# Staging the transposed attention weights: three buffers instead of two, one of them inside freed memory, and the pieces spread evenly over nineteen chunks

## The chip, the cores and the metric

The kernel runs on one core of a Trainium2 chip. The metric is device time in microseconds (us) of one execution. Before the change the median of eight executions is 3200.1 us (3193.46 to 3205.57). One execution was recorded by the hardware profiler; all rows of the profile below are from it.

The engines are named as in the profile: PE is TensorE's matmul, PEld its weight load, DVE is VectorE, ACT is ScalarE, POOL is GpSimd, SP is SyncE. SP, ACT and POOL also issue DMA transfers: the hardware queues of SP and ACT appear as q1 and q10, the software queue of POOL as q0.

## The reference, cut to what matters

The kernel computes the output and all gradients of one transformer block: a conditioned layer norm, recurrent attention over 64 segments of 32 tokens that carry 8 memory rows, a second conditioned layer norm, and a gated linear unit (GLU).

```python
# forward
h = layernorm(x) * (1 + ca) + sa
x = x + ga * attention(h, mem0, Wq, Wk, Wv, Wo)     # 64 segments, one after another
h2 = layernorm(x) * (1 + cb) + sb
hh = sigmoid(h2 @ w_gate) * (h2 @ w_up)
out = x + gb * (hh @ w_down)
# backward, the parts near the change (grad_out is given)
d_w_down = hh.T @ d_b                               # out_9
d_w_gate = h2.T @ d_g ;  d_w_up = h2.T @ d_u        # out_7, out_8
# and then the attention, from the last segment to the first; it needs
# Wo, Wv, Wk and Wq transposed
```

Sizes: 2048 tokens, model width 512, 32 heads of 128, GLU width 1792. Everything is bfloat16, and the sums are float32.

## The kernel before, in words

The program has phases: the forward attention (`phase2`), the GLU forward and backward by tiles of 128 tokens and after them the GLU's weight gradients (`phase3`), the backward attention (`phase4`), and the attention's weight gradients (`phase5`). The change lies in the last part of `phase3`, which the profile shows from about 1391 to 1587 us.

**The chunks.** This part computes weight gradients as long sums on TensorE: each output tile sums 16 matmuls, one for each tile of 128 tokens. First come eleven chunks of the gradient of `w_down` (fc = 3 to 13; `wd_chunk`, matmuls on L1141), each of 16 matmuls of 512 columns. Then come eight chunks of the GLU weight gradients (four of `w_gate`, four of `w_up`; L1211), each of 4 x 16 matmuls of 448 columns. That makes `n_chunks` = 19.

**The rings.** The operands are loaded into memory that the forward attention has left. `Wk` holds `dbr` in one half and `h2r` in the other. `Wv` (16384 elements per partition) holds a ring of two halves of 7168 elements: the chunks of HHROWS (1.5 MB), then of DGROWS and DUROWS (1.8 MB each). Their loads are issued on the ACT queue (L1137, L1187), each when the chunk that last read that half is done. The 2048 elements of `Wv` behind the ring are not used in this part. In the GLU tiles ahead they held two buffers of `grad_out` and two of the attention's rows.

**The pieces.** The backward attention needs `WoT`, `WvT`, `WkT` and `WqT`. `p4_weights_setup_pieces` makes 32 pieces, eight for each matrix in that order. A piece loads 0.5 MB of weights into a stage buffer (the load on L1265 or L1279), turns it with 16 transposes on TensorE in four groups of four (L1270 or L1283), and copies each group from PSUM with DVE or ACT (L63, L61). PSUM has two buffers for the groups (`wtp`). The stage pool has two buffers, so the load of a piece waits until the piece two before it has been turned. All 32 loads run on SP's queue, since `kk` is a multiple of 4 whenever a load is issued.

**The order.** After each chunk `emit_setup` emits two pieces until none is left: 22 behind the eleven chunks of `w_down`, and 10 behind the first five GLU chunks. The last three GLU chunks have none. The framework fixes each engine's order when the kernel is built: it takes instructions by their emission order and readiness, and an engine then executes its list strictly in that order. A group of transposes whose load is late therefore holds the matmuls listed behind it. The framework also sets the waits: a write into memory waits for the accesses before it that overlap it, and a new tile waits until the tiles that had the memory are released.

**Around it.** The store of the last tile of the GLU part (`DAOT`, L1121) and a reload from it (`daq`, L1243) are on SP's queue among the first piece loads. The first copy into `WoT` takes memory that this store reads. At the end the pools are closed, and the buffers of `phase4` (loads on L1405, L1408 and L1422, memsets on L1333, `RBd`, `dOT`) take the memory of `Wv`, `Wk` and the stages.

Of the kernel before, what the change touches and what calls it, by code (L numbers as in the profile page):

```python
# [7 lines left out]
BF16 = mybir.dt.bfloat16  # L8
# [32 lines left out]
class K:  # L41
# [856 lines left out]
    def phase3(self):  # L898
        nc, tc, cfg, io = self.nc, self.tc, self.cfg, self.io
        D, DC, F, FC, NT, T = cfg.D, cfg.DC, cfg.F, cfg.FC, cfg.NT, cfg.T  # L900
# [6 lines left out]
        d = self.dram  # L907
        with ExitStack() as ctx:
# [224 lines left out]
            kk = [0]  # L1133

            def load_hr(g):
                w = min(384, F - 384 * g)
                (nc.sync if g < 2 else nc.scalar).dma_start(hrs[g][:, :, 0:w], self.HHROWS[:, 384 * g:384 * g + w].rearrange("(j p) f -> p j f", p=128))  # L1137

            def wd_chunk(fc, ps, ot):
                for j in range(NT):  # L1140
                    nc.tensor.matmul(ps[:], lhsT=hrs[fc // 3][:, j, (fc % 3) * 128:(fc % 3) * 128 + 128], rhs=dbr[:, j, :],  # L1141
                                     start=(j == 0), stop=(j == NT - 1))
                self.evac("act" if kk[0] % 2 == 0 else "dve", ot[:], ps[:])
                kk[0] += 1
                nc.gpsimd.dma_start(io["out_9"][fc * 128:(fc + 1) * 128, :], ot[:])
# [22 lines left out]
        with ExitStack() as ctx:  # L1168
            op_ = ctx.enter_context(tc.tile_pool(name="p3g_o", bufs=2, reuse_waits="tile"))
            psG = ctx.enter_context(tc.tile_pool(name="p3g_ps", bufs=4, space=PSUM, reuse_waits="tile"))  # L1170
            setup_pieces = self.p4_weights_setup_pieces(ctx)
            n_chunks = 2 * NCH + FC - 3
            per_chunk = (len(setup_pieces) + n_chunks - 1) // n_chunks

            def emit_setup():
                for _ in range(per_chunk):
                    if setup_pieces:
                        setup_pieces.pop(0)()
            h2r = self.flat(self.Wk, NT * D, NT * D).rearrange("p (j d) -> p j d", j=NT)
            load_hr(2)  # L1180
            xrs = []

            def load_xr(i):
                if i < 2 * NCH:
                    rows, ch = ((self.DGROWS, self.DUROWS)[i // NCH], i % NCH)
                    t = ring[i % 2].rearrange("p (j f) -> p j f", j=NT)
                    nc.scalar.dma_start(t, rows[:, ch * CH:(ch + 1) * CH].rearrange("(j p) f -> p j f", p=128))  # L1187
                    xrs.append(t)

            for fc in range(3, FC):  # L1190
                wd_chunk(fc, psG.tile([128, D], F32, name="gps2", tag="g"), op_.tile([128, D], BF16, name="ot2", tag="o"))
                if fc == 4:
                    self.get_db(cfg.NS // 4 - 1)
                if fc == 5:
                    load_hr(3)
                elif fc == 8:
                    load_hr(4)
                elif fc == 9:
                    nc.scalar.dma_start(h2r, self.H2ROWS[:, :].rearrange("(j p) d -> p j d", p=128))
                elif fc == 11:  # L1200
                    load_xr(0)
                emit_setup()
            load_xr(1)
            k = kk[0]
            for (rows, outw) in ((self.DGROWS, io["out_7"]), (self.DUROWS, io["out_8"])):
                for ch in range(NCH):
                    xr = xrs.pop(0)
                    for c in range(DC):
                        ps = psG.tile([128, CH], F32, name="gps", tag="g")
                        for j in range(NT):  # L1210
                            nc.tensor.matmul(ps[:], lhsT=h2r[:, j, c * 128:(c + 1) * 128], rhs=xr[:, j, :],  # L1211
                                             start=(j == 0), stop=(j == NT - 1))
                        ot = op_.tile([128, CH], BF16, name="ot", tag="o")
                        self.evac("act" if k % 2 == 0 else "dve", ot[:], ps[:])
                        k += 1
                        nc.gpsimd.dma_start(outw[c * 128:(c + 1) * 128, ch * CH:(ch + 1) * CH], ot[:])
                    load_xr(NCH * (outw is io["out_8"]) + ch + 2)
                    emit_setup()
            while setup_pieces:
                setup_pieces.pop(0)()  # L1220
# [31 lines left out]
    def p4_weights_setup_pieces(self, ctx):  # L1252
        nc, tc, cfg, io = self.nc, self.tc, self.cfg, self.io
        D, DC, H, E = cfg.D, cfg.DC, cfg.H, cfg.E
        HB = 4
        stg = ctx.enter_context(tc.tile_pool(name="p4stage", bufs=2, reuse_waits="tile"))
        sps = ctx.enter_context(tc.tile_pool(name="p4sps", bufs=2, space=PSUM, reuse_waits="tile"))
        pieces = []
        kk = [0]

        def qkv_piece(src_ap, dst, h0):
            def f():
                srcv = src_ap.rearrange("(c p) h e -> p c h e", p=128)
                wn = stg.tile([128, DC, HB, E], BF16, name="wn", tag="s")
                (nc.sync if kk[0] % 2 == 0 else nc.gpsimd).dma_start(wn[:], srcv[:, :, h0:h0 + HB, :])  # L1265
                for hi in range(HB):
                    h = h0 + hi
                    tp = sps.tile([128, DC, 128], BF16, name="wtp")
                    for c in range(DC):
                        nc.tensor.transpose(tp[:, c, :], wn[:, c, hi, :], self.ident[:])  # L1270
                    self.evac("dve" if kk[0] % 3 != 2 else "act", dst[:, h, :], tp[:, :, :].rearrange("p c d -> p (c d)"))
                    kk[0] += 1
            return f

        def wo_piece(h0):
            def f():
                wov = io["A_Wo"].rearrange("h e d -> e h d")
                won = stg.tile([128, HB, D], BF16, name="won", tag="s")
                (nc.sync if kk[0] % 2 == 0 else nc.gpsimd).dma_start(won[:], wov[:, h0:h0 + HB, :])  # L1279
                for c in range(DC):  # L1280
                    tp = sps.tile([128, HB, 128], BF16, name="wtp")
                    for i in range(HB):
                        nc.tensor.transpose(tp[:, i, :], won[:, i, c * 128:(c + 1) * 128], self.ident[:])  # L1283
                    self.evac("dve" if kk[0] % 3 != 2 else "act", self.WoT[:, c, h0 * E:(h0 + HB) * E],
                              tp[:, :, :].rearrange("p i e -> p (i e)"))
                    kk[0] += 1
            return f

        for h0 in range(0, H, HB):
            pieces.append(wo_piece(h0))  # L1290
        for (src_ap, dst) in ((io["A_Wv"], self.WvT), (io["A_Wk"], self.WkT), (io["A_Wq"], self.WqT)):
            for h0 in range(0, H, HB):
                pieces.append(qkv_piece(src_ap, dst, h0))
        return pieces
# [725 lines left out]
```

The softmax here doesn't subtract the row's maximum and nothing guards it: scores larger than these inputs give would overflow.

## Time and profile before

| what | value |
|---|---|
| median of eight executions | 3200.1 us |
| the profiled execution: time, span | 3197.22 us, 3195.4 us |
| PE busy | 2985.6 us (93% of the span) |
| DVE, ACT, POOL busy | 1586.9, 1159.0, 1481.2 us |
| mean granted TensorE clock | 0.982 of full speed |
| DMA in the whole span | 726.12 MB, mean 227 GB/s |
| chunks of `w_down` and first GLU matmuls, 1391 to 1485 us | 23.19 MB, mean 247 GB/s |
| rest of the GLU weight gradients, 1485 to 1587 us | PE without idle time |

Times in a row are microseconds unless they are marked ns. A row of the timeline gives the start, the time to the end of the merged instructions, the engine, the line, what is written and read, the count, and in brackets the idle time of the engine before it with what ended it. A group `x4` of transposes is one of the four groups of a piece.

### The profile page before, as it was taken

How to read it: one execution, taken by the hardware profiler on the slowest of the kernel's cores; microseconds unless marked ns; L12 is line 12 of the kernel's file. 1: busy time of each engine (PE TensorE's matmuls, PEld its weight loads, DVE VectorE, ACT ScalarE, POOL GpSimd, SP SyncE). 2: the span in 40 equal slices, each digit the busy share in tenths (PEclk: the TensorE clock that was granted, in tenths of full speed). 3: DMA queues.
4: the chain of work that ended last, by engine and by line, in shares of the span. 5: the costliest groups of instructions: out<-in, count | busy, mean ns of one | idle time of the engine just before them, and what ended most of it. 6: DMA issues, size and time to landing. Idle time of an engine off the chain costs nothing.

```text
span 3195.4 us, 98797 instructions
## 1 busy us (share of the span) xinstructions
PE 2985.6 (93%) x39993; PEld 1727.7 (54%) x40069; DVE 1586.9 (50%) x3770; ACT 1159.0 (36%) x2829; POOL 1481.2 (46%) x2973
## 2 busy tenths in 40 slices
PE   5999999999998899988989999999999969999999
PEld 3666666666665444445555555555555534455454
DVE  4655666666655777633244545555555521323221
ACT  2454444444444333312144444444444410101011
POOL 3666666666664566521244444444444421333322
PEclk8999999999999999989999999999999989999999
DMA  9888888888788798887599999999999999998886
GB/s 296 204 211 202 203 202 207 202 203 211 196 203 245 180 220 216 218 255 233 184 222 253 261 256 267 271 267 262 269 256 272 261 223 221 239 207 206 203 229 154
DMA packets 958893, 726.12 MB, mean 227 GB/s; under 512 B 656019, under 2 KB 831139, under 8 KB 958309
## 3 DMA queue, kind: packets, MB, share of 16 engines
q1 hardware_dynamic: 827940, 508.77, 70.5%
q0 software_dynamic: 59056, 148.62, 13.9%
q10 hardware_dynamic: 71440, 62.40, 7.7%
q8 instruction: 316, 5.18, 0.7%
q14 instruction: 141, 1.15, 0.1%
HBM read 294.91 MB, written 276.33 MB: 179 GB/s over the span
## 4 chain that ended last, share of the span: by engine, by line
PE 41%; DMA 8%; issue 4%; ACT 2%; DVE 1%; POOL 1%; SPq 1%; ACTq 0%; DVEq 0%; POOLq 0%
PE dh_ps L212 10%; PE gps L1813 5%; PE pass_ps L249 4%; PE gps5o L1826 4%; PE g_ps L1502 4%; PE gps L1211 3%; PE dh_tps L212 3%; DMA rows<-DKR 2%; PE tps L1417 2%; PE dp_ps L1481 1%; ACT RAd L61 1%; PE dp_ps L1489 1%; DMA Kst<-KST 1%; PE dh_ft L318 1%; PE turn_ps L1383 1%
## 5 line engine op out<-in xcount | busy, mean ns | idle before, releaser
L1813 PE MATMUL gps<-rows,hrows 128*128 128x512 bf16 (+2 forms) x2124 | 415.7, 355 | 3.8 <-ACT ot L61 1.9
L1813 PEld LDWEIGHTS <-hrows 128*128 128x128 bf16 x2160 | 211.1, 98 | 206.7 <-issue 2.3
L249 PEld LDWEIGHTS <-hT 128*32 128x32 bf16 x6144 | 158.1, 97 | 161.4 <-issue 1.9
L1531 POOL COPY dOst<-RAd 96x512 bf16<-96x512 bf16 x128 | 78.5, 614 | 358.4 <-DVE RAd L63 347.5
L852 POOL TENSOR_TENSOR Pst<-Pst,rden 120x1408 bf16<-120x1408 bf16 x63 | 161.0, 2555 | 112.3 <-issue 78.8
L1817 POOL DMA_DIRECT2D out_dram<-ot x108 | 81.5, 755 | 227.8 <-DVE ot L63 140.3
L63 DVE CAST ot<-gps 128x512 bf16<-128x512 f32 (+3 forms) x76 | 47.9, 632 | 249.1 <-PE gps L1813 105.9
L309 DVE TENSOR_TENSOR dh_lo<-dh_ps,dh_hi 128x256 bf16<-128x256 f32 x128 | 48.4, 420 | 246.0 <-ACT dh_hi L305 246.0
L1826 PE MATMUL gps5o<-WoT,rows 128*128 128x512 bf16 x588 | 133.7, 387 | 25.3 <-DMA rows<-OSR 24.6
L61 ACT ACTIVATE ot<-gps 128x512 bf16<-128x512 f32 (+3 forms) x75 | 41.0, 548 | 282.8 <-PE gps L1813 106.6
L212 PE MATMUL dh_ps<-WvT,dVT 128*32 128x512 bf16 x2048 | 135.1, 381 | 0.0
L249 PE MATMUL pass_ps<-Wv,hT 128*32 128x512 bf16 x2048 | 133.5, 380 | 0.0
L249 PE MATMUL pass_ps<-WoT,dyT 128*32 128x512 bf16 x2048 | 123.6, 384 | 5.2 <-ACT dyT L1590 5.2
L1491 DVE SCALAR_TENSOR_TENSOR dS<-dp_ps,Pst_l 128x512 bf16<-128x512 f32 (+1 forms) x192 | 112.2, 640 | 32.3 <-PE dp_ps L1489 32.2
L220 PE MATMUL at_ps<-Wo,OT 128*32 128x256 bf16 x4096 | 124.6, 275 | 0.5 <-DVE OT L63 0.2
L249 PE MATMUL pass_ps<-Wk,hT 128*32 128x512 bf16 x2048 | 123.2, 382 | 1.5 <-ACT hT L842 1.1
L212 PE MATMUL dh_ps<-WkT,dKT 128*32 128x512 bf16 x2048 | 124.0, 383 | 0.1
L212 PE MATMUL dh_ps<-WqT,dQT 128*32 128x512 bf16 x2048 | 122.3, 379 | 0.1
L249 PE MATMUL pass_ps<-Wq,hT 128*32 128x512 bf16 x2048 | 121.8, 379 | 0.0
L61 ACT ACTIVATE dVT<-g_ps 128x512 bf16<-128x512 f32 (+1 forms) x192 | 107.8, 562 | 37.3 <-PE g_ps L1502 18.3
L63 DVE CAST RA0v<-pass_ps 128x512 bf16<-128x512 f32 x128 | 88.3, 690 | 65.7 <-PE pass_ps L249 61.2
L694 ACT ACTIVATE ET<-st_ps 128x480 bf16<-128x480 f32 (+1 forms) x192 | 96.1, 535 | 54.2 <-ACT qT L61 37.3
(407 smaller groups left out, 7038.8 us busy)
## 6 DMA issues: line engine op xcount, KB each, us to landing
OSR<-Ost SPq DMA_DIRECT2D x64, 352.0 KB
OT<-OT SPq DMA_DIRECT2D x64, 352.0 KB
VT<-VTr SPq DMA_DIRECT2D x64, 352.0 KB
PS<-Pst SPq DMA_DIRECT2D x64, 352.0 KB
OT_l<-OT SPq DMA_DIRECT2D x64, 352.0 KB
Pst_l<-PS SPq DMA_DIRECT2D x64, 352.0 KB
VT_l<-VT SPq DMA_DIRECT2D x64, 352.0 KB
DKR<-rows_x POOLq DMA_DIRECT2D x64, 352.0 KB, 5.8
```

The source lines that it names most:

```text
L61: return nc.scalar.activation(out, in_, AF.Copy)
L63: return nc.vector.tensor_copy(out, in_)
L212: self.nc.tensor.matmul(ps[32 * j:32 * j + 32, :], lhsT=lhsT, rhs=w, start=(n < 4), stop=(n >= total - 4), tile_position=(0, 32 * j))
L220: nc.tensor.matmul(ps[32 * j:32 * j + 32, :], lhsT=x[k], rhs=w[k][:, 256 * d:256 * d + 256], start=(n == 0), stop=(n == total - 1), tile_p ...
L249: self.nc.tensor.matmul(ps[32 * j:32 * j + 32, :], lhsT=lhs(c), rhs=rhs, start=(c == 0), stop=(c == DC - 1), tile_position=(0, 32 * j))
L694: nc.scalar.activation(part3(ET, pi)[:, 0:n, 0:120], st_ps[:, 0:n, 0:120], AF.Exp, scale=cfg.scale)
L852: nc.gpsimd.tensor_tensor(Pst[0:120, :, :], Pst[0:120, :, :], rden[:, :].unsqueeze(2).to_broadcast([120, G, 128]), op=ALU.mult)
L1211: nc.tensor.matmul(ps[:], lhsT=h2r[:, j, c * 128:(c + 1) * 128], rhs=xr[:, j, :], start=(j == 0), stop=(j == NT - 1))
L1491: nc.vector.scalar_tensor_tensor(out=part3(dS, pi), in0=ps[:, 0:n, :], scalar=cfg.scale, in1=part3(Pst, pi), op0=ALU.mult, op1=ALU.mult)
L1502: nc.tensor.matmul(ps[:, j, :], lhsT=lh[:, g * GW:(g + 1) * GW], rhs=rh[:, g * GW:(g + 1) * GW], start=True, stop=True)
L1813: nc.tensor.matmul(ps[:, 0:ng * E], lhsT=hrows[:, tp_, c * 128:(c + 1) * 128], rhs=rows[:, tp_, 0:ng * E], start=(tp_ == 0), stop=(tp_ == ...
L1826: nc.tensor.matmul(pss[gg][:], lhsT=rows[:, tp_, gg * E:(gg + 1) * E], rhs=dyrows[:, tp_, :], start=(tp_ == order[0]), stop=(tp_ == order[ ...
```

## The change

There are three stage buffers in place of two. Two are tiles of the pool `p4stage`, which takes the same memory as before. The third is the 2048 elements of `Wv` behind the ring. Pieces use the three in turn, beginning with the second: the piece numbered n from 1 takes buffer n modulo 3, so the pieces 2, 5, ... 32 use the one in `Wv`. The load of a piece waits for the piece three before it. The choice of the queue is gone from the code, and all loads are issued on SP.

The pieces are spread evenly over the 19 chunks: after the chunk numbered k, 32k/19 pieces (rounded up) have been emitted. That is 19 behind the eleven chunks of `w_down` (2, 4, 6, 7, 9, 11, 12, 14, 16, 17, 19) and 13 behind the eight GLU chunks (21, 22, 24, 26, 27, 29, 31, 32), with the last piece behind the last chunk.

```diff
             n_chunks = 2 * NCH + FC - 3
-            per_chunk = (len(setup_pieces) + n_chunks - 1) // n_chunks
+            n_setup, done = len(setup_pieces), [0]
 
             def emit_setup():
-                for _ in range(per_chunk):
-                    if setup_pieces:
-                        setup_pieces.pop(0)()
+                done[0] += 1
+                while setup_pieces and (n_setup - len(setup_pieces)) * n_chunks < done[0] * n_setup:
+                    setup_pieces.pop(0)()
...
-        stg = ctx.enter_context(tc.tile_pool(name="p4stage", bufs=2, reuse_waits="tile"))
+        stg = ctx.enter_context(tc.tile_pool(name="p4stage", bufs=1, reuse_waits="tile"))
...
+        slots = [stg.tile([128, DC * HB * E], BF16, name=f"stage{i}") for i in range(2)]
+        slots = [t[:, :] for t in slots] + [self.flat(self.Wv, 2 * cfg.NT * 448, DC * HB * E)]
+        np_ = [0]
+
+        def slot(pat, **kw):
+            np_[0] += 1
+            return slots[np_[0] % 3].rearrange(pat, **kw)
 
         def qkv_piece(src_ap, dst, h0):
             def f():
                 srcv = src_ap.rearrange("(c p) h e -> p c h e", p=128)
-                wn = stg.tile([128, DC, HB, E], BF16, name="wn", tag="s")
-                (nc.sync if kk[0] % 2 == 0 else nc.gpsimd).dma_start(wn[:], srcv[:, :, h0:h0 + HB, :])
+                wn = slot("p (c h e) -> p c h e", c=DC, e=E)
+                nc.sync.dma_start(wn, srcv[:, :, h0:h0 + HB, :])
...
-                won = stg.tile([128, HB, D], BF16, name="won", tag="s")
-                (nc.sync if kk[0] % 2 == 0 else nc.gpsimd).dma_start(won[:], wov[:, h0:h0 + HB, :])
+                won = slot("p (h d) -> p h d", h=HB)
+                nc.sync.dma_start(won, wov[:, h0:h0 + HB, :])
```

## The prediction

> **What bounds the kernel now.** I read the page first. TensorE is busy for 93% of the span, so a change counts where TensorE stands still or runs at a lower clock.
>
> ```profile
> span 3195.4 us, 98797 instructions
> PE 2985.6 (93%) x39993; PEld 1727.7 (54%) x40069; DVE 1586.9 (50%) x3770; ACT 1159.0 (36%) x2829; POOL 1481.2 (46%) x2973
> ```
>
> Second, TensorE's waits from 1391 to 1485 us, the stretch of the `w_down` chunks and the first GLU matmuls:
>
> ```profile
> PE wtp L1270 <- DMA wn<-in_A_Wk_dram: 6.6, 4, 3.9
> PE wtp L1283 <- DMA won<-in_A_Wo_dram: 5.1, 2, 4.9
> PE wtp L1270 <- DMA wn<-in_A_Wv_dram: 4.3, 4, 2.5
> PE wtp L1283 <- DVE WoT L63: 3.7, 1, 3.7
> ```
>
> The columns are total us, times, longest. Three rows are transposes that wait for their piece's load: 16.0 us in ten waits. The timeline gives them one by one: four long ones of 4.85, 2.53, 2.18 and 3.88 (13.4 together), and six short ones of 0.27, 0.49, 0.45, 0.87, 0.35 and 0.22. The fourth row is something else: the first copy into `WoT` waits for the store `DAOT`.
>
> Third, the timeline behind the longest wait, and a piece with no long wait for comparison:
>
> ```profile
> 1424.40 0.61 PE L1283 MATMUL wtp<-ident,won 128*128 128x128 bf16 x4 [4.85 <-DMA won<-in_A_Wo_dram]
> 1424.80 0.63 PE L1141 MATMUL gps<-Wk,Wv 128*128 128x512 bf16 x1
> 1425.23 0.63 PE L1283 MATMUL wtp<-ident,won 128*128 128x128 bf16 x4
> ...
> 1439.34 0.38 PE L1270 MATMUL wtp<-ident,wn 128*128 128x128 bf16 x4
> 1439.56 0.38 PE L1141 MATMUL gps<-Wk,Wv 128*128 128x512 bf16 x1
> 1439.77 0.39 PE L1270 MATMUL wtp<-ident,wn 128*128 128x128 bf16 x4
> ```
>
> A group of four and a matmul take 0.83 us from start to start in the first part and 0.43 us in the second: TensorE comes back from the wait at half its clock. The wait costs more than its length.
>
> Fourth, the busy time by stretches (length, PE busy, PEld, DVE, ACT, POOL, granted clock, DMA share, GB/s):
>
> ```profile
> 1424.00:1438.00 14.00, 11.20 (x74) 6.59 (x76) 4.00 (x9) 2.88 (x5) 1.09 (x2) 0.80 0.59 183
> 1438.00:1470.00 32.00, 26.99 (x234) 16.24 (x239) 12.51 (x29) 8.85 (x15) 2.17 (x4) 1.00 0.72 236
> 1485.00:1555.00 70.00, 70.00 (x467) 39.43 (x465) 16.35 (x36) 13.21 (x23) 10.67 (x20) 0.98 0.69 224
> 1555.00:1587.00 32.00, 32.00 (x177) 16.78 (x175) 3.96 (x7) 2.72 (x5) 5.59 (x11) 1.00 0.34 113
> ```
>
> While TensorE waits, the DMA engines are not full (shares of 0.59 and 0.72), so it is the time of one transfer that is waited for, and not their throughput. From 1485 on TensorE has no gap, with pieces (to 1555) or without.
>
> Fifth, what the long waits are made of. In the chain of waits a piece's load takes 3.44 to 4.60 us from issue to the transposes where it is alone, and 5.77 to 8.95 us at the four long waits. Just ahead of each of those, ACT's queue had issued a ring load (1412.72, 1430.18, 1457.76 and 1470.31). The load issued at 1415.40 moved nothing until 1419.2; in that window the queues show:
>
> ```profile
> q10 hardware_dynamic: 1200, 0.92, 81.5%
> q0 software_dynamic: 18, 0.06, 3.7%
> ```
>
> q1, the piece's queue, has no row: the ring load goes through first.
>
> **The change part by part.** The sum is made against the profiled execution, 3197.22 us (span 3195.4), which lies 2.9 us under the median of 3200.1; the difference found is taken from the median.
>
> *The third buffer* sends each load out one piece earlier against its need. A piece's period without the waits: 18 pieces lie between 1400.9 and 1469.2, and 68.3 us less the 12.0 us of waits in them is 56.3 us, or 3.1 us for one. Against that slack the waits become 4.85 - 3.1 = 1.75, 3.88 - 3.1 = 0.8, and nothing for the others: 2.6 us left of 16.0. Bounds: all 16.0 stay (if the loads only queue behind one another) or none. I take 4 us left, a little over the arithmetic, because pieces that come sooner also ask for their loads sooner. Gain 12.0 us.
>
> *The lower clock* behind the two longest waits goes with them. Behind 4.85 us, four groups and three matmuls (one has no record) take 2.96 us (1424.40 to 1427.36); at 0.22 us for each, as the full-clock rows have it, they take 1.54. The next seven matmuls take 2.63 instead of 1.51. Lost: 2.5 us. Behind 3.88 us, four groups and four matmuls take 3.17 instead of 1.64, and the 32 matmuls behind them 7.33 instead of 6.05 (0.189 each). Lost: 2.8 us. Behind 2.53 us nothing was lost, as the rows from 1439.34 show; so once the waits are under that, the whole 5.3 us goes. Bounds 0 and 5.3; I take 5.3, since the waits left are 1.75 and less.
>
> *Throughput*: does the third load only fill a full pipe? In the 94 us from 1391 to 1485 23.19 MB were moved. Without the 16.0 + 5.3 us and with three pieces fewer (3 us, 1.6 MB), 21.6 MB move in 70 us: 309 GB/s. Full slices of this stretch show 355 to 385 GB/s. It fits, with 13% to spare.
>
> *The spread* takes three pieces (48 transposes, 12 copies) out of the `w_down` stretch, where they are waited for, and puts them into the GLU chunks, where TensorE is the bound: some 1.0 us of TensorE each (four groups at 0.22 plus the changes between kinds), the same in both places, so zero. DVE and ACT stay under a quarter busy there (16.35 and 13.21 of 70), which hides the copies. If that cover went, each copy would cost its 0.43 us (DVE) or 0.60 us (ACT).
>
> *The last piece* now has no chunk behind it to fill its gaps. Two PSUM buffers take two groups in 0.44 us; then each further group waits for a copy (0.43 or 0.60 us and about 0.3 to be noticed twice). That is about 2.2 us where the groups alone cost 0.9: 1.3 us more. What is queued behind: the `phase4` tiles in `Wv` (`RBd`, `dOT`, the three loads on SP from 1587.51). TensorE idles 5.80 us there anyway for `dOst`, whose DMA goes out behind three memsets of 1.29 us on POOL that wait for the last GLU matmul alone; they hide some 0.7 us. Bounds 0 (hidden wholly) and 2.5; I take 1.5 with the late loads.
>
> *The start.* The second piece's load now goes into memory that held `grad_out` until about 1386.4 instead of going out at 1383.4; its need is at 1401.5, so that is free. But SP issues in order: the store `DAOT` (1389.60) may come to lie behind one or two piece loads, and behind the 2 MB load of H2ROWS on ACT's queue (1391.62). The first copy into `WoT` waits for it, and TensorE with it (3.67 us before). Bounds: 0, and 2.1 MB at 360 GB/s = 5.8 us. I take 1.5, one load of 0.52 MB, since a load that is ready at 1386.4 leaves SP ahead of 1389.60. POOL's queue is not moved past; the queue choice and the fixed tiles change no instruction (every load of before is an SP row).
>
> Sum: -12.0 - 5.3 + 1.5 + 1.5 = -14.3 us, so 3183 us for the profiled execution and 3186 us for the median.
>
> One rule of the Trainium skill speaks against the row on q1: "DMA: Bandwidth & Descriptors", section "Queues, rings and completion order", says that each DMA engine takes turns between the queue rows that have work. By it a piece's load would get half of the engines at once beside a ring load, and none of the long waits would outlast a third buffer: the sum would be 4 us lower, about 3182 us. The same page ("Issuing engines are not separate DMA queues") says that queues share the same 16 engines, so that a third transfer in flight adds no bandwidth; the throughput row above weighs that, and the measured rows decide.
>
> **The rivals.**
>
> *A, the loads stay late* (0.15). With three loads asked for, piece loads and ring loads stand in one line, and the wait moves to the piece behind. For it: q1's missing row. Against: shares of 0.59 and 0.72. If 10 of the 16.0 us stay, and one of the two clock drops: -6.0 - 2.7 + 3 = -5.7, 3194.5 us.
>
> *B, nothing comes of it* (0.05). TensorE's order is fixed at build time; if it puts the pieces earlier by as much as the loads come earlier, the waits stay: 3200 us. Against: the trace places pieces directly behind their chunk.
>
> *C, slower* (0.12). The third buffer is part of the tile `Wv`. If its waits are drawn for the tile and not for the elements, the load of each of the eleven pieces in it waits for the chunk that reads the ring, and the next chunk waits for that load: 11 x 4.0 us (the middle of 3.44 and 4.60) = 44 us, 3230 us with part of the gain. It turns the sign past (14.3 + 6.4) / 4.0, so past five such waits. Against: the ring load issued at 1470.31 went into one half of `Wv` while TensorE read the other without a wait.
>
> **How the numbers follow.** Forecast 0.68: 3186, own range 3180 to 3193. About 0.2% (6.4 us) can be told from no change. Faster by more: the forecast and a fifth of A, 0.71. Within: the rest of A and B, 0.17. Slower: C, 0.12. The range 3179 to 3200 reaches from the forecast with all bounds good (-16.0 - 5.3 = 3179) past A to B; it leaves out C and little else.
>
> **What would show it.** Right: the long waits for `wn` and `won` are gone or under 2 us, the granted clock between 1420 and 1485 is near 1.00, the last `w_down` matmul comes some 15 us sooner, the gap before the first `dOst` matmul is still near 6 us. Wrong: matmuls on L1141 or L1211 that wait for a DMA (C), a wait for `WoT` well over 3.7 us (the start), transposes that wait as long at other pieces (A).

## The result, and the profile after

The changed kernel takes 3185.37 us (median of 21 executions, 3178.27 to 3196.03). The kernel before, run beside it, takes 3204.09 us (median of 62), 4 us more than the eight executions shown before the change. The ratio is 0.9945, with a 95% interval of 0.9935 to 0.9955: 17.6 us faster, between 14.4 and 20.8 (the two medians themselves lie 18.7 us apart).

The page of the changed kernel, whose profiled execution took 3187.13 us:

```profile
span 3185.2 us, 98793 instructions
PE 2982.5 (94%) x39993; PEld 1730.2 (54%) x40069; DVE 1582.0 (50%) x3770; ACT 1159.9 (36%) x2829; POOL 1481.8 (47%) x2973
```

TensorE issues the same matmuls (x39993). Over the whole span its busy time falls by 3.1 us and its idle time by 7.1. The waits that the change aims at went almost wholly. TensorE's waits from 1391 to 1485 us, in total us, times, longest:

```profile
PE wtp L1290 <- DVE WoT L63: 3.1, 1, 3.1
PE wtp L1277 <- DMA Wv<-in_A_Wv_dram: 1.4, 1, 1.4
...
PE wtp L1290 <- DMA Wv<-in_A_Wo_dram: 0.6, 1, 0.6
PE wtp L1290 <- DMA stage<-in_A_Wo_dram: 0.4, 1, 0.4
PE gps L1211 <- DMA Wv<-DGROWS: 0.2, 1, 0.2
```

The ten waits for pieces were 16.0 us; three are left, 2.4 us together. Two of them are at the buffer in `Wv` (the load is named `Wv<-in_A_...`, those of the pool `stage<-in_A_...`; L1277 and L1290 are the former L1270 and L1283). The wait for `WoT` is still there, 3.1 us after 3.7. The last row is new and small: a GLU matmul waits 0.2 us for its ring load.

The stretches of the changed kernel (columns as before the change):

```profile
1424.00:1438.00 14.00, 12.36 (x107) 7.49 (x108) 5.85 (x14) 4.24 (x8) 1.37 (x3) 1.00 0.83 265
1438.00:1470.00 32.00, 31.42 (x230) 17.87 (x232) 9.85 (x22) 8.04 (x14) 3.79 (x7) 1.00 0.83 276
1470.00:1485.00 15.00, 15.00 (x103) 8.48 (x102) 3.27 (x7) 2.88 (x5) 2.17 (x4) 1.00 0.71 229
```

From 1424 to 1438 the granted clock is 1.00 where it was 0.80, and the DMA engines work at a share of 0.83 where they stood at 0.59. From 1470 to 1485 TensorE has no gap.

For each profiled execution below, one number measures the part that the change touches: the time from the first matmul of the first chunk to the first matmul on `dOst` in `phase4` (here called the part). It was 207.95 us before (1391.27 to 1599.22) and is 187.43 us after (1393.37 to 1580.80): 20.5 us less. Kernels profiled twice differ by 1.2 to 1.6 us in it. The time from there to the end of the span scatters between 1594 and 1608 us over the thirteen profiles of this study, whatever the kernel; the span of this execution is therefore only 10.2 us shorter. The medians, with 6 to 21 executions of each changed kernel, average that out.

| kernel | part, us | waits for piece loads, us | against the kernel before: ratio (95% interval) |
|---|---|---|---|
| before | 207.95 | 16.0 | 1 |
| changed | 187.43 | 2.4 | 0.9945 (0.9935 to 0.9955) |
| changed, repeated | 188.98 | 3.2 | 0.9947 (0.9927 to 0.9967) |
| third buffer alone | 194.05 | 6.9 | 0.9955 (0.994 to 0.997) |
| spread alone | 199.54 | 11.7 | 0.9984 (0.9972 to 0.9996) |
| over 18 chunks | 192.36 | 5.7 | 0.9949 (0.9932 to 0.9967) |
| late start | 192.82 | 2.4 | 0.996 (0.9945 to 0.9974) |
| weighted order | 189.46 | 0 | 0.9933 (0.9906 to 0.9959) |
| weighted order, repeated | 190.64 | 0 | 0.9947 (0.9927 to 0.9968) |
| weighted order, two buffers | 206.67 | 14.9 | 1.002 (1.0004 to 1.0036) |
| weighted order, later reload | 181.50 | 0 | 0.9917 (0.9892 to 0.9942) |
| changed, later reload | 190.18 | 2.4 | 0.9942 (0.992 to 0.9964) |

### The profile page after: what moved, and what is told of

It reads as the page before. It is cut to its first block, busy times and chain, and to the rows that moved or that the text cites. A ratio compares the mean times of both kernels' runs of the same rounds, so it can differ in the third digit from the quotient of the medians.

```text
span 3185.2 us, 98793 instructions
## 1 busy us (share of the span) xinstructions
PE 2982.5 (94%) x39993; PEld 1730.2 (54%) x40069; DVE 1582.0 (50%) x3770; ACT 1159.9 (36%) x2829; POOL 1481.8 (47%) x2973
## 4 chain that ended last, share of the span: by engine, by line
PE 36%; DMA 8%; issue 8%; ACT 2%; POOL 2%; DVE 1%; SPq 1%; ACTq 0%; POOLq 0%; DVEq 0%
PE dh_ps L212 9%; PE gps L1820 7%; PE pass_ps L249 4%; PE g_ps L1509 3%; PE gps5o L1833 3%; PE dh_tps L212 2%; DMA rows<-DKR 2%; PE tps L1424 2%; DMA rows<-OSR 1%; PE dp_ps L1488 1%; DMA Kst<-KST 1%; ACT RAd L61 1%; PE dp_ps L1496 1%; PE dh_ft L318 1%; PE turn_ps L1390 1%
```

## The experiments

The theory is that of the prediction: TensorE waits for the time of one transfer, and one more buffer covers it. Its rivals are that throughput limits, so that the spread carries the gain, and that the long waits have another cause than the ring loads.

### The third buffer alone

```diff
-                done[0] += 1
-                while setup_pieces and (n_setup - len(setup_pieces)) * n_chunks < done[0] * n_setup:
-                    setup_pieces.pop(0)()
+                for _ in range(per_chunk):
+                    if setup_pieces:
+                        setup_pieces.pop(0)()
```

> The third buffer alone: two pieces behind each chunk, as in the kernel before, but three stage buffers, the third in Wv. Theory (the wait is the time of one transfer, and one more buffer covers it): the waits of transposes for their loads fall from 16.0 us to about 4, both drops of the clock go, and the last piece still has three chunks behind it, so -14 to -18 us against the kernel before. Rival (throughput: two pieces for each chunk of 16 matmuls ask for more than the queues bring beside the ring loads, and only the spread cures that): 8 us or more of waits stay, at other pieces, with at least one drop of the clock, and the gain is -3 to -9 us.

Measured: 0.9955, so -14.4 us (-9.6 to -19.2), and a part of 194.05 us. The waits of TensorE from 1391 to 1485 us:

```profile
PE wtp L1290 <- DVE WoT L63: 3.3, 1, 3.3
PE wtp L1290 <- DMA stage<-in_A_Wo_dram: 2.1, 1, 2.1
PE wtp L1277 <- DMA stage<-in_A_Wv_dram: 1.8, 1, 1.8
PE wtp L1290 <- DMA Wv<-in_A_Wo_dram: 1.5, 1, 1.5
PE wtp L1277 <- DMA stage<-in_A_Wk_dram: 0.8, 1, 0.8
...
PE wtp L1277 <- DMA Wv<-in_A_Wk_dram: 0.7, 1, 0.7
```

The gain is the theory's. But 6.9 us of waits stay, not the 4 of the theory and nearly the 8 of the rival. No single wait is over 2.1 us, and the granted clock stays nearer full (0.93 from 1424 to 1438, 0.98 from 1438 to 1470). By the part, the buffer carries most of the gain, and not all of it: 13.9 us of 19.0 to 20.5.

### The spread alone

```diff
-            per_chunk = (len(setup_pieces) + n_chunks - 1) // n_chunks
+            n_setup, done = len(setup_pieces), [0]
 
             def emit_setup():
-                for _ in range(per_chunk):
-                    if setup_pieces:
-                        setup_pieces.pop(0)()
+                done[0] += 1
+                while setup_pieces and (n_setup - len(setup_pieces)) * n_chunks < done[0] * n_setup:
+                    setup_pieces.pop(0)()
```

> The spread alone: the pieces evenly over 19 chunks, with two stage buffers of the pool as before. Theory (the buffer carries the gain): every load that goes out behind a ring load is still late, at least 11 of the 16.0 us stay and one of the two drops of the clock, and the last piece behind the last chunk costs 1.4 us: -1 to -5 us. Rival (the spread carries it): half of the waits or less stay, -9 us or better.

Measured: 0.9984, so -5.1 us (-1.3 to -9.0), and a part of 199.54 us. The waits of TensorE, same stretch:

```profile
PE wtp L1283 <- DMA won<-in_A_Wo_dram: 5.0, 2, 4.8
PE wtp L1270 <- DMA wn<-in_A_Wv_dram: 3.5, 2, 2.3
PE wtp L1283 <- DVE WoT L63: 3.4, 1, 3.4
PE wtp L1270 <- DMA wn<-in_A_Wk_dram: 3.2, 1, 3.2
```

With two buffers the long waits behind the ring loads stay (4.77, 2.32 and 3.18 us by the timeline). What the spread takes away is the last long wait, the 3.88 us one behind the second load of DGROWS, with the clock that it cost (1470 to 1485 us has no gap here), and some short ones. This is the theory's case: 11.7 of the 16.0 us stay, and so does the drop of the clock behind the longest (0.78 from 1424 to 1438). Of the two changes alone, -13.9 and -8.4 us in the part, the sum is -22.3; together they give -20.5 and -19.0 in two profiles. They add up, nearly.

### The ring loads as the cause of the long waits

```diff
-                if fc == 5:
-                    load_hr(3)
-                elif fc == 8:
-                    load_hr(4)
-                elif fc == 9:
+                if fc == 9:
```

This is made on the kernel before. It leaves out two loads of HHROWS, and five chunks read what the ring held before.

> The kernel before without two of the ring loads (HHROWS for the chunks 9 to 11 and 12 to 13): these five chunks of the gradient of w_down read what the ring held before, so five blocks of 128 rows of that output are not the reference's. Theory (the long waits are piece loads that stand behind a ring load): the waits of 4.85 us near 1424 and 2.53 us near 1438 are gone or under 1 us, the clock stays up there, while the waits of 2.18 and 3.88 us behind the loads of DGROWS stay within 1 us. Rival (the pieces' own rate is too high): waits of 2 us and more stay between 1405 and 1445.

The waits from 1391 to 1485 us:

```profile
PE wtp L1266 <- DMA wn<-in_A_Wk_dram: 6.1, 2, 3.9
PE wtp L1279 <- DMA won<-in_A_Wo_dram: 3.8, 2, 3.1
PE wtp L1279 <- DVE WoT L63: 3.3, 1, 3.3
PE wtp L1266 <- DMA wn<-in_A_Wv_dram: 0.8, 2, 0.6
```

The two waits whose ring loads are gone fall from 4.85 and 2.53 us to 0.63 and 0.56. The two behind DGROWS stay at 2.15 and 3.95 (2.18 and 3.88 before). So these long waits are made by the ring loads; the part is 199.89 us, 8.1 less than before, in a single execution. A wait of 3.13 us that was only 0.27 before appears at 1404.41, at the third piece, just ahead of the stretch that the rival named. Its load was issued at 1397.4, while ACT's queue still moved H2ROWS, with the small packets of `daq` ahead of it on SP's queue. That it has the same cause is likely and was not tried.

Leaving the loads out also lowers the traffic (195 instead of 259 GB/s from 1400 to 1424), so this run alone doesn't tell a late start from a share of the engines. The queues show both. In the changed kernel, a piece's load issued at 1415.30, behind the ring load of 1412.87, moved nothing until 1419.2; the queues in that window:

```profile
q10 hardware_dynamic: 1496, 1.15, 91.7%
q0 software_dynamic: 44, 0.12, 7.8%
```

But the ring load is not through by then: in the kernel before, 1.00 MB of its 1.57 MB (1536 KB) had moved when the piece's load began at 1419.2, and in the changed kernel 1.22 MB. From there on the two move side by side. The queues of the kernel before from 1464.5 to 1466.5, behind the first load of DGROWS:

```profile
q1 hardware_dynamic: 399, 0.41, 57.4%
q10 hardware_dynamic: 401, 0.36, 51.4%
```

So a ring load costs a piece's load twice. The first packet comes late: 2.8 to 3.9 us after the issue at the four long waits, against 1.0 us for the loads of 1440.19 and 1446.05, which had no ring load ahead. Then the engines are shared. What holds the first packet back is not shown.

In the changed kernel the load of 1415.30 belongs to a piece that is needed only at 1423.30, and TensorE waits 0.60 us for it, where the load behind the same ring load cost 4.85 us before.

### The last piece at the end

```diff
-                while setup_pieces and (n_setup - len(setup_pieces)) * n_chunks < done[0] * n_setup:
+                while setup_pieces and (n_setup - len(setup_pieces)) * (n_chunks - 1) < done[0] * n_setup:
```

> The changed kernel with the pieces spread over the first 18 chunks, so that the last piece has a GLU chunk behind it that fills its gaps. Theory: TensorE's first matmul on dOst comes 1.0 to 1.5 us sooner after the last GLU matmul (11.9 us instead of 13.3 from the start of the last 16 transposes), and the median is that much lower, which can hardly be told from the changed kernel: -17 to -20 us against the kernel before. Rival (the gap there hides the last piece wholly): no difference in that stretch.

The end of the changed kernel, on TensorE:

```profile
1567.54 0.61 PE L1277 MATMUL wtp<-ident,Wv 128*128 128x128 bf16 x8
1568.74 0.61 PE L1277 MATMUL wtp<-ident,Wv 128*128 128x128 bf16 x8 [0.60 <-DVE WqT L63]
...
1580.80 0.59 PE L1509 MATMUL g_ps<-Pst_l,dOst 128*128 128x128 bf16 x4 [5.46 <-DMA dOst<-RBd]
```

From the first matmul behind the last GLU matmul to the first on `dOst` it takes 13.26 us (1567.54 to 1580.80), and in the kernel over 18 chunks 12.09 (1570.33 to 1582.42): 1.2 us, inside the theory's range. The last piece waits once, 0.60 us, for a PSUM buffer. Since the 16 transposes cost about 0.9 us wherever they stand, the place costs some 0.3 us. The kernel as a whole is no faster (0.9949, -16.3 us), and its part is 3 to 5 us longer, with waits for loads of 5.7 us instead of 2.4 and 3.2. Two of these, of 2.07 and 2.06 us, were followed by half speed on TensorE; after the second the granted clock from 1438 to 1470 is 0.95, where the changed kernel has 1.00. It has 20 instead of 19 pieces behind the `w_down` chunks; that this one piece makes the difference was not tried by itself.

### A later start, for the wait for WoT

```diff
-                while setup_pieces and (n_setup - len(setup_pieces)) * n_chunks < done[0] * n_setup:
+                while setup_pieces and (n_setup - len(setup_pieces)) * (n_chunks - 1) < (done[0] - 1) * n_setup:
```

> The changed kernel with no piece behind the first chunk: the 32 pieces evenly over the last 18. Theory (the wait for WoT is a wait for the store of DAOT, which lands near 1400 whatever the pieces do, and TensorE idles only because the first pieces are listed ahead of the next chunk): the second chunk's 16 matmuls (3.5 us) fill the time, the wait for WoT falls under 1 us and the clock stays up behind it, 3 to 6 us sooner in the stretch; the pieces are packed a little closer, which gives up to 2 us back: -18 to -24 us against the kernel before. Rival (the clock and the start of the loads only shift): the waits for loads grow by as much, -15 to -18 us.

> The changed kernel once more, unchanged, on the chip of the three kernels beside it, to compare them with it. -17 to -20 us against the kernel before; the waits for loads again under 4 us together, the wait for WoT again 3.0 to 3.7 us.

The repeated kernel has 0.9947, -17.0 us, with 3.2 us of waits for loads, as expected; the wait for `WoT`, 4.0 us, is a little over the 3.7. The later start has 0.996 (-12.8 us; -8.3 to -17.6): worse than both theories said, though the interval reaches into the rival's range. The first wait for `WoT` does fall, from 3.1 to 0.31 us, so the matmuls of the second chunk cover what the first copy into `WoT` waits for. That this is the store of `DAOT` is named by the profile only in the kernel before. In the changed kernel it names a load of HHROWS, and in its repeat, the two changes alone and the kernel over 18 chunks the store of `accs` into `DMOD`, another store of the GLU part. The copy starts 0.6 to 1.2 us after the reload of `DAOT` goes out in all of these, so several transfers end close together, and which one counts is open. But a new wait of 6.79 us stands at the third piece, also for a copy into `WoT`.

### Pieces where their loads have time

```diff
-                done[0] += 1
-                while setup_pieces and (n_setup - len(setup_pieces)) * n_chunks < done[0] * n_setup:
+            plan = [0, 2] + [1] * (FC - 5) + [3] * (2 * NCH - 1) + [0]
...
+                for _ in range(plan.pop(0)):
                     setup_pieces.pop(0)()
```

> The changed kernel with the pieces laid where TensorE has time to spare for their loads: none behind the first chunk, two behind the second, one behind each of the nine chunks of w_down that follow, three behind each of the first seven GLU chunks, none behind the last. Theory (each piece needs 3 to 5 us for its load, so 11 pieces beside 3.5 us of matmuls each are covered, and 21 beside 12 us are covered too): no wait for a load over 0.5 us, the wait for WoT under 1 us, the granted clock at 1.00 from the first chunk to the end of the stretch, and no last piece at the end: 6 to 10 us sooner than the changed kernel, -23 to -28 us against the kernel before. Rival (three pieces in a row behind a GLU chunk meet the 1.8 MB ring loads): waits of 2 us and more at the third pieces in the GLU chunks, -14 to -19 us.

> The kernel with the weighted order, unchanged, on the same chip, to compare with: -18 to -24 us against the kernel before; the wait for WoT near 1413 again 6 to 7 us, and no wait for a piece's load over 0.5 us.

No wait for a piece's load is left in either profile, as the theory had it, and three pieces in a row behind a GLU chunk wait for nothing. But the two comparisons gave 0.9933 and 0.9947 (-21.4 and -17.0 us), less than expected both times and hardly better than the changed kernel, because the wait of 6.6 us (7.1 in the repeat) for `WoT` stands here too. What makes it is a chain over three engines, here in the order of time:

```profile
1405.54 0.29 POOL L1249 COPY dyb<-daq 128x128 bf16<-128x128 bf16 x1 [10.34 <-DMA daq<-DAOT]
...
1406.19 1.08 POOL L1145 DMA_DIRECT2D out_dram<-ot  x2
1412.09 0.69 DVE L63 CAST ot<-gps 128x512 bf16<-128x512 f32 x1 [8.32 <-DMA out_dram<-ot]
1412.70 0.41 DVE L63 COPY WoT<-wtp 128x512 bf16<-128x512 bf16 x1
...
1413.16 0.58 PE L1289 MATMUL wtp<-ident,stage 128*128 128x128 bf16 x4 [6.60 <-DVE WoT L63]
```

POOL's list has the copies from `daq` ahead of two output stores, and `daq` is the reload of `DAOT`. The stores go out at 1406.19. Only when they have landed is a buffer of `ot` free for the third chunk's output tile, which DVE copies at 1412.09. The copy into `WoT` is behind that on DVE, and TensorE is behind the copy.

The next kernels move the reload and what POOL copies from it behind the chunk fc = 8. `pin` ties the order of SP and POOL in this stretch to the order of emission, so that the framework can't take these copies earlier.

```diff
-            xrs = []
+            xrs, i1 = [], len(self.traced())
...
-                if fc == 4:
-                    self.get_db(cfg.NS // 4 - 1)
+                if fc == 8:
+                    self.get_db(cfg.NS // 4 - 1), self.pin(i1, [ET.SP, ET.Pool])
```

> The kernel with the weighted order, and the reload of DAOT (daq) with the copies from it on POOL (dyb, dyT) behind the chunk fc = 8 instead of ahead of the third chunk's store. TensorE's order is the same. Theory (the 6.6 us wait for WoT at 1413 is a chain: POOL waits for daq, the stores of two output tiles stand behind it on POOL's queue, the copy of the third output tile on DVE waits for its buffer, and the copies into WoT stand behind that on DVE): the chain is cut, no wait of TensorE over 1 us is left between 1391 and 1570, the clock is at 1.00 there, and the stretch from the first chunk to the first matmul on dOst falls from 189.5 us by 7 to 10: -25 to -31 us against the kernel before. Rival (the third output tile's store is late by itself, 6 us on the queues): the wait stays over 3 us, -19 to -23 us.

> The changed kernel with the reload of DAOT and its copies on POOL behind the chunk fc = 8. Theory (with two pieces behind the first chunk TensorE waits for the store of DAOT itself, which this does not move, and the later chain is covered by the pieces): the wait for WoT stays at 3 to 4 us and the time at -16 to -20 us against the kernel before. Rival (the reload on SP's queue ahead of the fourth piece's load is what makes the changed kernel's first pieces late): 3 us and more better than that.

On the weighted order this gives 0.9917 (0.9892 to 0.9942), 26.6 us less than before, with a median of 3173.49 us; the part falls to 181.50 us, 26.5 less. The waits of TensorE from 1391 to 1485 us are now:

```profile
PE wtp L1289 <- ACT WoT L61: 0.8, 2, 0.6
PE wtp L1289 <- DVE WoT L63: 0.6, 1, 0.6
PE gps L1141 <- DMA Wv<-HHROWS: 0.4, 1, 0.4
PE gps L1210 <- DMA Wv<-DGROWS: 0.3, 1, 0.3
```

What is late next are the ring loads themselves, by 0.4 and 0.3 us, with 344 GB/s moved from 1391 to 1424 us. This version is the fastest of the study. Its interval against the kernel before overlaps that of the changed kernel (0.9935 to 0.9955) a little. Beside it, the weighted order without the later reload had a median of 3185.19 us and the changed kernel with it 3183.25; the parts, 181.5 against 187.4 and 189.0 us for the changed kernel, separate them too.

On the changed kernel the later reload does nothing (0.9942; the wait for `WoT` at 3.7 us, waits for loads at 2.4 us), as the theory expected. Its wait for `WoT` is the one at the first piece, ahead of the chain, and no wait of TensorE comes out of the chain itself. That it is the store of `DAOT`, as the theory has it, is not shown: the profile names the load of HHROWS here too.

### The weighted order with two buffers

> The kernel before, with its two stage buffers, and the pieces laid as in the kernel with the weighted order. Theory (what counts is the time between a buffer's release and its next need; spacing gives it in the w_down chunks, but the third piece of three in a row behind a GLU chunk has only its own load time): in the w_down chunks waits of 2 us or less in all, in the GLU chunks seven third pieces, whose waits the framework's order fills with matmuls: -15 to -24 us against the kernel before. Rival (the buffer is needed whatever the spacing): at least 8 us of waits for loads stay, -5 to -12 us.

This is the plan of the weighted order on the kernel before. Measured: 1.002 (1.0004 to 1.0036), 6.4 us slower than before (1.3 to 11.5), where even the rival had a gain. The part is no longer than before, 206.67 us against 207.95; where the 6.4 us come from is not shown. In the `w_down` chunks the waits for loads fall to 3.9 us, where 2 or less were expected. From 1485 us on, where the kernel before has none, they are:

```profile
PE wtp L1269 <- DMA wn<-in_A_Wq_dram: 5.9, 2, 3.4
PE wtp L1269 <- DMA wn<-in_A_Wk_dram: 5.1, 3, 1.9
```

These are five waits in five chunks, 1.5 to 3.4 us each: with two buffers, the third piece of three in a row can be loaded only when the first has been turned, and its transposes are listed ahead of matmuls that could run. With three buffers the same order waits for nothing. So order and buffers are one question: here a run of three pieces needed three buffers. Other lengths were not tried.

## Why the prediction held, and where it was off

The predicted 3186 us met 3185.4, partly since the kernel before ran 4 us slower in the longer comparison than in the executions shown. The difference is the better measure: -14.3 us was forecast, and -17.6 (-14.4 to -20.8) measured, in the part -20.5 and -19.0. By its steps:

- **The third buffer: 12.0 us.** 16.0 us of waits fell to 2.4 and 3.2, so 13.6 and 12.8 us went; the arithmetic's 2.6 us left was closer than the 4 that I rounded it to. The mechanism is shown: the two waits whose ring loads were left out went, and with two buffers and an even spread three of the four long waits stay. The weighted order covers most of them with two buffers too, at the price of waits elsewhere. One reading in it was too strong: the ring load does not go through first, it delays the start of the piece's load and then shares the engines with it.
- **The lower clock: 5.3 us.** It went: 1.00 from 1424 to 1485 us in both profiles of the changed kernel. The condition that I gave for it, waits under 2.53 us, is no rule: behind waits of 2.07 (over 18 chunks) and 2.12 us (third buffer alone) the clock fell. That a wait of 2.28 us in the repeat left it at full speed was luck.
- **The spread: zero. This step failed.** I reckoned only where TensorE's work stands, and not that fewer pieces beside the ring loads leave each load more time. Alone it took 8.4 us off the part and 5.1 us (1.3 to 9.0) off the kernel. On top of the third buffer it took the waits from 6.9 to 2.4 and 3.2 us, and from the part 5.1 to 6.6 us; in the medians 0.9955 and 0.9945 can't be told apart. The 12.0 us that I gave to the buffer needed both.
- **The start: +1.5 us.** It cost nothing that can be seen: the wait for `WoT` was 3.1, 4.0 and 3.7 us in three profiles of kernels with this start, and 3.7 before. SP issued two loads at 1385.05 and that into `Wv` at 1388.62, all ahead of the store of `DAOT` at 1391.63, as the step had it. But the store lost no time by it: from its issue to that of its reload it took 8.7 us, 9.0 in the repeat, and 9.1 before.
- **The last piece: +1.5 us.** 1.2 us in that gap, of which 0.9 only moved there: about 0.3.
- **Throughput.** The transfers did fit. The changed kernel moves 316, 265, 276 and 229 GB/s in the stretches from 1400 to 1485, a mean of 277 where I had estimated 309, and no `w_down` or GLU matmul waited longer than 0.2 us for a ring load.

The two smaller costs and the waits left, 1.5 + 1.2 + 0.8 to 1.6 us too high together, cover the 3.3 us between forecast and measurement. The rest of the part's -19.0 to -20.5 us, up to some 2 us, no step had. Behind the wait for `WoT` the granted clock from 1400 to 1424 was 0.93 in both profiles of the changed kernel and 0.86 before, which is 24 x 0.07 = 1.7 us; but it was 0.90 with the same start and the later reload, so this can't be put down to the change.

Rival A (loads stay late, the wait moves on) is the state of the third buffer alone in a weak form: 6.9 us in shorter waits, with a granted clock of 0.93 from 1424 to 1438. B fell with the waits. C fell: the only wait of a GLU or `w_down` matmul for a load in the changed kernel was 0.2 us, and pieces in `Wv` were loaded while TensorE read the ring.

The rule of the Trainium skill ("DMA: Bandwidth & Descriptors", "Queues, rings and completion order": the DMA engines take turns between queue rows with work) agrees with these runs once both queues move: 399 packets on q1 against 401 on q10. What the prediction drew from it, half of the engines at once, does not: a load on q1 moved nothing for its first 3.9 us, in both kernels, while a ring load issued 2.4 to 2.7 us earlier on q10 moved. The traces don't show whether q1 already counted as a row with work in that time.

## What to carry to other kernels

A short load that must be in time behind long ones needs cover for its own time and for that of the long one ahead of it: one more buffer, or fewer short loads beside it. Count the buffers against the longest run of loads that the order puts in a row, since the same order gained with three buffers and gained nothing with two. And when a wait goes, follow the in-order lists of the other engines to what stands next: here one reload, waited for on POOL's list, held 6.6 us that came out only when the waits ahead of it were gone.

## What the runs showed of the hardware that was not expected

- A load behind one on another hardware queue began late, and the two then shared the engines: a 0.5 MB load on q1 behind a 1.5 MB load on q10 moved its first packet 3.9 us after its issue, where 1.0 us is what loads with no ring load ahead took. Behind the first load of DGROWS the two then moved 399 and 401 packets in 2 us.
- TensorE's clock: the length of a wait alone doesn't tell what it does. Behind waits of 2.53 us (before), 2.28 (changed, repeated) and even 3.18 (spread alone) it stayed at full speed, eight transposes in 0.62 us or four in 0.40. Behind waits of 2.07 us (over 18 chunks) and 2.12 (third buffer alone) it was at half speed at once, eight in 1.02 and 1.03 us. Behind one of 2.40 us (changed, later reload) it fell 1.3 us after the wait's end, four in 0.61 us at 1425.05. The time at half speed differs as much. Behind the wait for `WoT` it was slow for some 7 us in the kernel before (1399.87 to 1406.8), and for 3 us in the changed kernel (1401.43 to 1404.6), after nearly the same wait.
